# A shorter fallback path, 33 extra products at the head and smaller stores of one chunk in a fused attention and feed-forward kernel

## The chip, the cores and the metric

The kernel runs on one core of one Trainium2 chip. The core has five engines with instruction streams of their own: TensorE (PE in the profile, its weight loads PEld), VectorE (DVE), ScalarE (ACT), GpSimd (POOL) and SyncE (SP), and 16 DMA engines that all queues share. The metric is the device time of one execution in microseconds (us), smaller is better. Before the change the median of three runs is 411.15 us, the lowest 410.89 us, the highest 411.72 us.

## What is computed

Attention over 8 batches and 8 heads of 64 dimensions. Keys and values have 1152 positions; queries are averaged in pairs first, so there are 576 queries per head. The attended values of the 8 heads, side by side, are the 512 features of 4608 tokens, which then pass through a multiplicative feed-forward block.

```python
q_pool = q.reshape(B, H, S // 2, 2, D).mean(axis=3)
scores = scale * np.matmul(q_pool, k.transpose(0, 1, 3, 2))
attn = softmax(scores)            # with the row's maximum taken off, and 1e-9 added to its sum
x = np.matmul(attn, v)            # -> (4608 tokens, 512)
a, b = x @ w1, x @ w2             # (512, 1024) each
out = ((a * b) @ w3) @ w_out      # (1024, 1024), (1024, 512) -> float32 (4608, 512)
```

## The kernel before, in words

**The main path.** Heads are worked two at a time: 32 pairs, numbered `p`. The scores of a pair go through PSUM buffers `psc` (line 438); ACT takes their exponential into `ring` without taking off a maximum (line 443). `av_mm` (line 456) multiplies 128 queries at a time with the values, to which a column of 1/16 is joined, so that PSUM holds the sum of the exponentials too; DVE divides by it (`av_norm`, line 486). The result must lie with its features on the partitions (`xT`). For the first eight pairs and for short tail groups PE turns it; for the others `x_dma` (line 476) issues one transposing DMA on SP's queue for each pair. The feed-forward block works on chunks of 512 tokens, nine of them, numbered 0 to 8: `w3 @ w_out` is multiplied once into `T16`, and each chunk is the products with `w1` and `w2`, their elementwise product `gT`, and the product with `T16` (`moe_groups`, line 592). A beam search (`_visits`, line 179) lays out beforehand in which order PE takes scores, values and the pieces of chunks. `LATE` is 7: chunks 0 to 6 are done as just said, in the gaps between scores; chunks 7 and 8 come last (`late_chunks`, line 672), in an order written out by hand, `LATE_ORDER`, with seven block products where a plain block scheme has eight. Their sums of blocks of `xT` are formed on POOL by `x_sums` (line 659).

**Stores.** `put` (line 619) scales a finished 128-token tile into an `osb` buffer, of which there are three, and `store` (line 581) writes it to HBM with one DMA. Chunks 0 to 4 use POOL's queue, chunks 5 and 6 SP's. The outputs of chunks 7 and 8 are stored in half tiles from `room`, on SP's or on ACT's queue (`LATE_BY_ACT`, line 257). DMAs of SP and ACT take eight completion semaphores, the lanes HW0 to HW7, in turn; a DMA waits on its queue until the one before it on its lane has landed.

**The guard.** Since no maximum is taken off, the sums must lie in a range for the half-precision result to be good. Lines 988 to 1009 count those that do; `bad` is the number that don't, and every engine loads it into a register (line 1007, in `late_chunks` after 8 of its units). After everything else each engine meets a branch (line 1010): if `bad` is zero it jumps over the code of `_general` (line 24), the fallback, which does the whole computation again with the maximum taken off, in loops over batch, 96-query chunk, pair of heads, and blocks of 128 features of the feed-forward block. With this case's data `bad` is zero and nothing of the fallback runs, but its instructions lie in each engine's stream between the branch and its target. At the target each engine waits for what is still under way. SP waits for the stores: first for some lanes one by one (a block at line 1010), then for all queues' lanes in a list of twelve instructions (line 1037); then the engines meet at a barrier.

**The head.** `first_loads` (line 386) starts the DMAs of the first pair. POOL writes the identity `ident16` (lines 843 to 847); PE's first work is `first_turn` (line 415), which turns the first blocks of keys and queries with it when they have come and POOL and DVE have cast them.

Of the kernel before, what the change touches and what calls it, by code (L numbers as in the profile page):

```python
# [8 lines left out]
FP32 = mybir.dt.float32  # L9
FP16 = mybir.dt.float16  # L10
AF = mybir.ActivationFunctionType
ALU = mybir.AluOpType
# [11 lines left out]
def _general(tc, q, k, v, out, w1sb, w2sb, T16):  # L24

    nc = tc.nc
    B, H, S, D = q.shape
    Sq = S // 2
    NJ = S // 128
    dm = H * D  # L30
    dff = w1sb.shape[2]
    NC = dm // 128
    NF = dff // 128
    QP = 96
    SCALE = 0.5 * float(D) ** -0.5
    SCL = 16.0
    W = 384
    kf, vf = (t.rearrange("b h s d -> (b h) s d") for t in (k, v))
    qr = q.rearrange("b h s d -> (b h s) d")
    with tc.tile_pool(name="gen", bufs=1) as sb, \  # L40
         tc.tile_pool(name="gen_ps", bufs=1, space=bass.MemoryType.PSUM) as ps, \
         tc.For_i(0, B, 1) as ib, tc.For_i(0, Sq, QP) as iq:
        xT = sb.tile([128, NC * QP], FP16)
        gT = sb.tile([128, NF * QP], FP16)
        with tc.For_i(0, H // 2, 1) as ip:
            pav = ps.tile([128, 512], FP32, tag="g_pav")
            for u in range(2):
                ih = ib * H + ip * 2 + u
                hs = u * 64
                kst = sb.tile([128, NJ, D], FP32, tag="g_kst")  # L50
                nc.gpsimd.dma_start(out=kst, in_=kf[bass.ds(ih, 1)].rearrange("o (c p) d -> p (o c) d", p=128))
                vst = sb.tile([128, NJ, D], FP32, tag="g_vst")
                nc.gpsimd.dma_start(out=vst, in_=vf[bass.ds(ih, 1)].rearrange("o (c p) d -> p (o c) d", p=128))
                qst = sb.tile([QP, 2, D], FP32, tag="g_qst")
                nc.gpsimd.dma_start(out=qst, in_=qr[bass.ds(ih * S + iq * 2, 2 * QP)].rearrange("(p t) d -> p t d", t=2))
                kh = sb.tile([128, NJ, 128], FP16, tag="g_kh")
                qh = sb.tile([QP, 128], FP16, tag="g_qh")
                vh = sb.tile([128, NJ, D], FP16, tag="g_vh")
                nc.gpsimd.memset(kh, 0.0)
                nc.gpsimd.memset(qh, 0.0)  # L60
                nc.gpsimd.tensor_copy(out=kh[:, :, 0:D], in_=kst)
                nc.gpsimd.tensor_tensor(out=qh[:, 0:D], in0=qst[:, 0, :], in1=qst[:, 1, :], op=ALU.add)
                nc.gpsimd.tensor_copy(out=vh, in_=vst)
                kT = sb.tile([128, NJ, 128], FP16, tag="g_kT")
                nc.sync.dma_start(out=kT, in_=kh.rearrange("p c d -> p (c d)"), transpose=True)
                qT = sb.tile([128, QP], FP16, tag="g_qT")
                nc.sync.dma_start(out=qT, in_=qh, transpose=True)
                kTf = kT.rearrange("p c i -> p (c i)")
                pss = ps.tile([128, S // W, 512], FP32, tag="g_pss")
                for w in range(S // W):  # L70
                    nc.tensor.matmul(pss[0:QP, w, 0:W], qT, kTf[:, w * W:w * W + W], start=True, stop=True)
                mx = sb.tile([QP, 1], FP32, tag="g_mx")
                nc.vector.tensor_reduce(out=mx, in_=pss[0:QP, :, 0:W], axis=mybir.AxisListType.XY, op=ALU.max)
                nb = sb.tile([QP, 1], FP32, tag="g_nb")
                nc.scalar.mul(out=nb, in_=mx, mul=-SCALE)
                e = sb.tile([QP, S // W, W], FP32, tag="g_e")
                nc.scalar.activation(out=e, in_=pss[0:QP, :, 0:W], func=AF.Exp, bias=nb, scale=SCALE)
                z = sb.tile([QP, 1], FP32, tag="g_z")
                nc.vector.tensor_reduce(out=z, in_=e, axis=mybir.AxisListType.XY, op=ALU.add)
                nc.vector.tensor_scalar(out=z, in0=z, scalar1=1e-9, scalar2=None, op0=ALU.add)  # L80
                rz = sb.tile([QP, 1], FP32, tag="g_rz")
                nc.vector.reciprocal(out=rz, in_=z)
                eh = sb.tile([QP, S], FP16, tag="g_eh")
                nc.vector.tensor_scalar(out=eh, in0=e.rearrange("p w i -> p (w i)"), scalar1=rz, scalar2=SCL,
                                        op0=ALU.mult, op1=ALU.mult)
                eT = sb.tile([128, NJ, QP], FP16, tag="g_eT")
                nc.sync.dma_start(out=eT, in_=eh, transpose=True)
                for jt in range(NJ):
                    nc.tensor.matmul(pav[hs:hs + 64, 0:QP], vh[:, jt, :], eT[:, jt, :], start=(jt == 0), stop=(jt == NJ - 1))
                nc.vector.tensor_copy(out=xT[hs:hs + 64, bass.ds(ip * QP, QP)], in_=pav[hs:hs + 64, 0:QP])  # L90
        with tc.For_i(0, NF, 1) as ift:
            pw = [ps.tile([128, 512], FP32, tag=tg, name=tg) for tg in ("g_pa", "g_pb")]
            for wt, p, tg in ((w1sb, pw[0], "g_w1"), (w2sb, pw[1], "g_w2")):
                wc = sb.tile([128, NC, 128], FP16, tag=tg, name=tg)
                nc.gpsimd.tensor_copy(out=wc, in_=wt[:, :, bass.ds(ift * 128, 128)])
                for mc in range(NC):
                    nc.tensor.matmul(p[:, 0:QP], wc[:, mc, :], xT[:, mc * QP:mc * QP + QP],
                                     start=(mc == 0), stop=(mc == NC - 1))
            asb = sb.tile([128, QP], FP32, tag="g_asb")
            nc.scalar.copy(out=asb, in_=pw[0][:, 0:QP])  # L100
            nc.vector.tensor_tensor(out=gT[:, bass.ds(ift * QP, QP)], in0=pw[1][:, 0:QP], in1=asb, op=ALU.mult)
        po = ps.tile([128, 512], FP32, tag="g_po")
        for ft in range(NF):
            nc.tensor.matmul(po[0:QP, :], gT[:, ft * QP:ft * QP + QP], T16[:, ft, :], start=(ft == 0), stop=(ft == NF - 1))
# [156 lines left out]
def kernel(  # L261
# [26 lines left out]
    QM = 4  # L288
    QT = Sq - QM * 128
    E1 = D + 1  # L290
    SCALE = 0.5 * float(D) ** -0.5
    SCL = 16.0
# [12 lines left out]
    ps = fast.enter_context(tc.tile_pool(name="ps", bufs=1, space=bass.MemoryType.PSUM))  # L305
# [4 lines left out]
    ident16 = const.tile([128, 128], FP16)  # L310
# [267 lines left out]
                nc.tensor.matmul(pw[:, d0:d0 + n], wt[:, mc, ft * 128:ft * 128 + 128], xT[:, mc, a:a + n],  # L578
                                 start=(mc == 0 and d0 == 0), stop=(mc == NC - 1), skip_group_check=True)

    def store(eng, pos, osb, cols=slice(0, dm)):
        b, r = pos // (2 * Sq) * 2, pos % (2 * Sq)
        if r == QM * 128:
            for u in range(2):
                r0 = (b + u) * Sq + QM * 128
                eng.dma_start(out=out[r0:r0 + QT, cols], in_=osb[u * QT:u * QT + QT, :])
            return
        if r > QM * 128:
            b, r = b + 1, r - QM * 128 - 2 * QT
        eng.dma_start(out=out[b * Sq:b * Sq + QM * 128, :].rearrange("(p c) n -> p c n", c=QM)[:, r // 128, cols], in_=osb)  # L590

    def moe_groups(c):
        t = {}
# [243 lines left out]
    def w_load(dst, src):  # L837
# [204 lines left out]
```

## Time and profile before

| what | us |
|---|---|
| median of three runs | 411.15 |
| the profiled execution's own time | 411.33 |
| its span, first to last instruction of the kernel | 409.7 |
| PE busy | 394.7 (96%) |
| ACT busy | 335.2 (82%) |
| DVE busy, POOL busy | 218.6 (53%), 213.0 (52%) |
| first product of PE starts | 5.16 |
| last arithmetic (DVE, line 764) ends | 404.65 |

The profile shows one execution on the chip. The span begins with the kernel's first instruction; the time outside it, 1.6 us here, is start and end of the program. "Busy" is the share of the span in which an engine works on something; waits, branches and DMA issues are not counted. The chain of waits goes back from the last instruction to what released it, step by step. A line number is one of the kernel's file before the change.

### The profile page before, as it was taken

The numbers are of one execution on the slowest core, as the hardware profiler recorded it, in microseconds if no ns is written. First come the engines' busy times: TensorE is split into PE (matmuls) and PEld (weight loads), VectorE is DVE, ScalarE is ACT, GpSimd is POOL, SyncE is SP. The second block draws the span as 40 slices with busy tenths as digits, with TensorE's granted clock in tenths as the row PEclk, the third lists the DMA queues.
The fourth block names the chain that finished last, engine by engine and source line by source line (L and its number), as shares of the span: only waits on it lengthen the run. The fifth ranks groups of instructions, "written<-read, shape, count | busy, mean of one in ns | idle before, by whom it ended". The sixth has DMA issues, their size and how long they took to land.

```text
span 409.7 us, 13103 instructions
## 1 busy us (share of the span) xinstructions
PE 394.7 (96%) x5473; PEld 260.2 (64%) x5473; DVE 218.6 (53%) x594; ACT 335.2 (82%) x380; POOL 213.0 (52%) x237
## 2 busy tenths in 40 slices
PE   3899999999999999999999999999999999999994
PEld 1477777566555655565556555665777655658883
DVE  1255664665455534554365536563456435856982
ACT  4978979898889998999999998998998989017752
POOL 5879976570555145604533346333533997070850
PEclk9999999999999999999999999999999999999999
DMA  8999999999599899949999999998997270020015
GB/s 255 252 308 284 267 282 313 342 241 271 195 226 237 214 290 283 282 47 251 311 242 260 239 286 280 256 284 199 282 232 185 28 149 14 15 91 27 2 39 172
DMA packets 92224, 86.35 MB, mean 211 GB/s; under 512 B 59776, under 2 KB 66176, under 8 KB 92160
## 3 DMA queue, kind: packets, MB, share of 16 engines
q1 hardware_dynamic: 82624, 60.11, 62.2%
q0 software_dynamic: 8384, 24.06, 20.4%
q10 hardware_dynamic: 1152, 1.31, 1.0%
q8 instruction: 43, 0.70, 0.7%
q14 instruction: 21, 0.17, 0.1%
HBM read 67.11 MB, written 9.44 MB: 187 GB/s over the span
## 4 chain that ended last, share of the span: by engine, by line
PE 93%; ACT 2%; DVE 2%; DMA 1%; issue 1%; ACTq 0%
PE psc L438 20%; PE avb L469 17%; PE mo L578 15%; PE mo L616 11%; PE mot L578 9%; PE b L713 7%; PE mo L556 3%; PE avb L466 3%; ACT ring L443 2%; PE b L616 2%; PE ptk L378 2%; PE mo L713 1%; DMA qst<-in_q_dram 1%; PE avb L713 1%; DVE kqT L380 1%; PE mot L556 1%
## 5 line engine op out<-in xcount | busy, mean ns | idle before, releaser
L443 ACT ACTIVATE ring<-psc 128x1024 f16<-128x1024 f32 x324 | 308.2, 1025 | 33.2 <-PE psc L438 31.4
L469 PEld LDWEIGHTS <-ring 128*128 128x128 f16 x2304 | 84.4, 98 | 26.3 <-issue 7.1
L438 PE MATMUL psc<-kqT 64*128 64x512 f16 (+7 forms) x1152 | 96.1, 290 | 3.6 <-ACT ring L443 0.9
L469 PE MATMUL avb<-vaug,ring 128*128 128x65 f16 x2304 | 91.4, 193 | 0.0
L350 POOL CAST kq<-kst 128x1152 f16<-128x1152 f32 x31 | 35.7, 1152 | 77.8 <-DMA kqT<-kq 56.7
L438 PEld LDWEIGHTS <-kqT 64*128 64x128 f16 x1152 | 45.9, 95 | 31.0 <-issue 8.5
L616 PE MATMUL mo<-T,gT 128*128 128x512 f16 x192 | 45.6, 380 | 0.0
L490 DVE RECIPROCAL rzall<-avb 128x2 f32<-128x2 f32 x144 | 23.8, 165 | 37.0 <-PE avb L469 20.3
L625 DVE TENSOR_SCALAR osb<-mo 128x512 f32<-128x512 f32 x24 | 16.6, 692 | 48.6 <-PE mo L616 48.6
L354 POOL TENSOR_TENSOR kq<-qst 128x512 f16<-128x512 f32 x31 | 39.4, 1271 | 2.3 <-DMA qst<-in_q_dram 2.3
L363 POOL CAST vaug<-vst 128x1152 f16<-128x1152 f32 x32 | 36.6, 1145 | 7.0 <-DMA vst<-in_v_dram 7.0
L609 DVE TENSOR_TENSOR gT<-mo,asb 128x512 f16<-128x512 f32 x36 | 24.9, 692 | 24.7 <-PE mo L578 24.6
L590 POOL DMA_DIRECT2D out_dram<-osb x18 | 9.9, 552 | 54.1 <-DVE rzall L490 54.1
L578 PE MATMUL mo<-xT,w2sb 128*128 128x512 f16 (+2 forms) x168 | 37.2, 350 | 0.0
L616 PEld LDWEIGHTS <-gT 128*128 128x128 f16 x224 | 19.8, 98 | 25.6 <-issue 5.2
L578 PEld LDWEIGHTS <-w2sb 128*128 128x128 f16 x256 | 21.9, 97 | 20.8 <-issue 4.2
L605 DVE COPY asb<-mo 128x512 f32<-128x512 f32 x32 | 22.1, 691 | 24.0 <-PE mo L578 23.7
L578 PEld LDWEIGHTS <-w1sb 128*128 128x128 f16 x256 | 22.0, 97 | 20.3 <-issue 3.9
L578 PE MATMUL mo<-xT,w1sb 128*128 128x512 f16 (+2 forms) x148 | 33.1, 352 | 0.0
L504 DVE TENSOR_TENSOR xb<-avb,rzall 128x128 f16<-128x128 f32 x96 | 28.0, 291 | 3.3
L578 PE MATMUL mot<-xT,w1sb 128*128 128x512 f16 (+1 forms) x104 | 23.6, 354 | 0.1
L578 PE MATMUL mot<-xT,w2sb 128*128 128x512 f16 (+1 forms) x84 | 19.5, 359 | 0.0
(141 smaller groups left out, 429.6 us busy)
## 6 DMA issues: line engine op xcount, KB each, us to landing
vst<-in_v_dram SPq DMA_DIRECT2D x25, 576.0 KB, 5.0
kst<-in_k_dram SPq DMA_DIRECT2D x23, 576.0 KB, 5.8
qst<-in_q_dram SPq DMA_DIRECT2D x23, 512.0 KB, 7.4
kst<-in_k_dram POOLq DMA_DIRECT2D x8, 576.0 KB, 9.8
out_dram<-osb POOLq DMA_DIRECT2D x18, 256.0 KB, 6.2
qst<-in_q_dram POOLq DMA_DIRECT2D x8, 512.0 KB, 10.5
vst<-in_v_dram POOLq DMA_DIRECT2D x7, 576.0 KB, 7.1
w3c<-in_moe_w_dram POOLq DMA_DIRECT2D x4, 512.0 KB, 8.2
```

The costliest lines, as they stand in the source:

```text
L350: nc.gpsimd.tensor_copy(out=kq16[:, 0:NJ].rearrange("p c u d -> p u c d"), in_=kst.rearrange("p u (c d) -> p u c d", d=D))
L354: eng.tensor_tensor(out=kq16[:, NJ:NJ + QM].rearrange("p c u d -> p u c d"), in0=qv[:, :, :, 0], in1=qv[:, :, :, 1], op=ALU.add)
L363: nc.gpsimd.tensor_copy(out=va[:, :, :, 0:D], in_=vs.pop(p).rearrange("p u (c d) -> p u c d", d=D))
L438: nc.tensor.matmul(psc[:, u, f - s * G:f - s * G + ln], kT2[u * 64:u * 64 + 64, jt, :], qpT[u * 64:u * 64 + 64, i0:i0 + ln], start=True, s ...
L443: nc.scalar.activation(out=ring[:, :, r0:r0 + G], in_=psc, func=AF.Exp, bias=0.0, scale=SCALE)
L469: nc.tensor.matmul(avb[:, o + u * E1:o + u * E1 + E1], ring[:, u, c0:c0 + 128], va[:, u, jt, :], start=(jt == 0 and u == 0), stop=(jt == N ...
L490: nc.vector.reciprocal(out=rzall[:, i, :], in_=av[:, :, D:E1].rearrange("p u o -> p (u o)"))
L504: nc.vector.tensor_tensor(out=xbt, in0=av[:, :, 0:D], in1=rzall[:, i, :].unsqueeze(2).to_broadcast([128, 2, D]), op=ALU.mult)
L578: nc.tensor.matmul(pw[:, d0:d0 + n], wt[:, mc, ft * 128:ft * 128 + 128], xT[:, mc, a:a + n], start=(mc == 0 and d0 == 0), stop=(mc == NC - ...
L609: nc.vector.tensor_tensor(out=t["g"][:, ft, :], in0=pb, in1=t["a"], op=ALU.mult)
L616: nc.tensor.matmul(po, t["g"][:, ft, tt:tt + 128], T16[:, ft, :], start=(ft == 0), stop=(ft == NF - 1))
L713: nc.tensor.matmul(pt[:, n * f:n * f + n], l[:, i, :], b[:, i, :], start=(p in (1, 5) and f == 0 and i == 0), stop=(i == kc - 1), skip_gro ...
```

## The change

Three things are edited.

1. `_general`, the fallback: its loop over heads and its loop over feature blocks are gone, so that three nested loops are left. A pass of the inner one now does both heads of a pair at once, with one transposing DMA for both heads' keys, one for the queries and one for the attention weights; the feed-forward block is done in one go for the 96 queries.
2. At the head PE multiplies the identity with its first 64 columns 33 times, into `avb`, right after POOL has the identity.
3. The stores of chunk 6 are cut: where one DMA wrote a tile of 128 rows x 512 columns, four write 128 columns each for the first two tiles, and eight write 64 rows x 128 columns each for the other two. That makes 24 DMAs of 4.

```diff
-    def store(eng, pos, osb, cols=slice(0, dm)):
+    def store(eng, pos, osb, cols=slice(0, dm), rows=slice(0, 128)):
...
-        eng.dma_start(out=out[b * Sq:b * Sq + QM * 128, :].rearrange("(p c) n -> p c n", c=QM)[:, r // 128, cols], in_=osb)
+        eng.dma_start(out=out[b * Sq:b * Sq + QM * 128, :].rearrange("(p c) n -> p c n", c=QM)[rows, r // 128, cols], in_=osb)
...
-                store(nc.sync if c >= LATE - 2 else nc.gpsimd, c * CH + tt, osb)
+                if c == LATE - 1:
+                    cut = 128 if tt < 256 else 64
+                    for r in range(0, 128, cut):
+                        for n in range(0, dm, 128):
+                            store(nc.sync, c * CH + tt, osb[r:r + cut, n:n + 128], slice(n, n + 128), slice(r, r + cut))
+                else:
+                    store(nc.sync if c == LATE - 2 else nc.gpsimd, c * CH + tt, osb)
...
+    for _ in range(33):
+        nc.tensor.matmul(avb[:, 0:64], ident16, ident16[:, 0:64], start=True, stop=True)
     for t in kq16s:
         nc.gpsimd.memset(t[QT:128, NB - 1], 0.0)
```

The core of the fallback's edit, cut to the loops:

```diff
         with tc.For_i(0, H // 2, 1) as ip:
-            for u in range(2):
-                ih = ib * H + ip * 2 + u
...
-                nc.sync.dma_start(out=kT, in_=kh.rearrange("p c d -> p (c d)"), transpose=True)
-                nc.sync.dma_start(out=qT, in_=qh, transpose=True)
...
-                nc.sync.dma_start(out=eT, in_=eh, transpose=True)
+            ih = ib * H + ip * 2
...
+            nc.sync.dma_start(out=kT, in_=kh.rearrange("p c o d -> p (c o d)"), transpose=True)
+            nc.sync.dma_start(out=qT, in_=qh.rearrange("p u o d -> p (u o d)"), transpose=True)
...
+            nc.sync.dma_start(out=eT.rearrange("p u c i -> p (u c) i"), in_=eh.rearrange("p u s -> p (u s)"), transpose=True)
...
-        with tc.For_i(0, NF, 1) as ift:
...
+        for m, wt in enumerate((w1sb, w2sb)):
+            for n in range(2):
                 for mc in range(NC):
+                    nc.tensor.matmul(pw[0:QP, m, n, :], xT[:, mc * QP:mc * QP + QP], wt[:, mc, n * 512:n * 512 + 512],
                                      start=(mc == 0), stop=(mc == NC - 1))
```

In the built programs' instruction lists, counted on each engine from the program's first instruction, the guard's branch and its target stand here (the order of all other instructions of the main path is the same, except that lanes are dealt out anew behind the added DMAs):

| engine | branch before | target before | branch after | target after |
|---|---|---|---|---|
| PE | 10951 | 11146 | 11017 | 11182 |
| SP | 334 | 508 | 356 | 485 |
| ACT | 719 | 836 | 720 | 808 |
| DVE | 680 | 810 | 681 | 774 |
| POOL | 371 | 542 | 371 | 499 |

The last four stores, all on ACT's queue, have lanes HW0 to HW3 before and HW4 to HW7 after.

More of the change, by code (lines that the diff above doesn't have):

```diff
@@ L43, in _general @@
         xT = sb.tile([128, NC * QP], FP16)
[L44 removed]
         with tc.For_i(0, H // 2, 1) as ip:
[L46 removed]
+            ih = ib * H + ip * 2
+            kst = sb.tile([128, NJ, 2, D], FP32, tag="g_kst")
+            vst = sb.tile([128, NJ, 2, D], FP32, tag="g_vst")
             for u in range(2):
[L48 to L90 removed]
@@ L91, in _general @@
-        with tc.For_i(0, NF, 1) as ift:
[L92 to L95, printed above, removed]
+                for st, src in ((kst, kf), (vst, vf)):
+                    nc.gpsimd.dma_start(out=st[:, :, u], in_=src[bass.ds(ih + u, 1)].rearrange("o (c p) d -> p (o c) d", p=128))
@@ new lines, in _general @@
+            for u in range(2):
+                nc.gpsimd.tensor_tensor(out=qh[:, u, u], in0=qst[:, u, 0], in1=qst[:, u, 1], op=ALU.add)
+            nc.gpsimd.tensor_copy(out=vh, in_=vst)
+            kT = sb.tile([128, NJ, 128], FP16, tag="g_kT")
+            nc.sync.dma_start(out=kT, in_=kh.rearrange("p c o d -> p (c o d)"), transpose=True)
+            qT = sb.tile([128, 2, QP], FP16, tag="g_qT")
+            nc.sync.dma_start(out=qT, in_=qh.rearrange("p u o d -> p (u o d)"), transpose=True)
@@ new lines, in _general @@
+            kTf = kT.rearrange("p c i -> p (c i)")
+            pss = ps.tile([128, 2, S // W, 512], FP32, tag="g_big", name="g_pss")
+            for u in range(2):
+                for w in range(S // W):
+                    nc.tensor.matmul(pss[0:QP, u, w, 0:W], qT[:, u, :], kTf[:, w * W:w * W + W], start=True, stop=True)
+            mx = sb.tile([QP, 2], FP32, tag="g_mx")
+            nc.vector.tensor_reduce(out=mx, in_=pss[0:QP, :, :, 0:W], axis=mybir.AxisListType.XY, op=ALU.max)
+            nb = sb.tile([QP, 2], FP32, tag="g_nb")
@@ new lines, in _general @@
+            nc.scalar.mul(out=nb, in_=mx, mul=-SCALE)
+            e = sb.tile([QP, 2, S // W, W], FP32, tag="g_e")
+            for u in range(2):
+                nc.scalar.activation(out=e[:, u], in_=pss[0:QP, u, :, 0:W], func=AF.Exp, bias=nb[:, u:u + 1], scale=SCALE)
+            z = sb.tile([QP, 2], FP32, tag="g_z")
+            nc.vector.tensor_reduce(out=z, in_=e, axis=mybir.AxisListType.XY, op=ALU.add)
+            nc.gpsimd.tensor_scalar(out=z, in0=z, scalar1=1e-9, scalar2=None, op0=ALU.add)
@@ new lines, in _general @@
+            rz = sb.tile([QP, 2], FP32, tag="g_rz")
+            nc.vector.reciprocal(out=rz, in_=z)
+            eh = sb.tile([QP, 2, S], FP16, tag="g_eh")
+            for u in range(2):
+                nc.gpsimd.tensor_scalar(out=eh[:, u], in0=e[:, u].rearrange("p w i -> p (w i)"), scalar1=rz[:, u:u + 1],
+                                        scalar2=SCL, op0=ALU.mult, op1=ALU.mult)
+            eT = sb.tile([128, 2, NJ, QP], FP16, tag="g_eT")
+            nc.sync.dma_start(out=eT.rearrange("p u c i -> p (u c) i"), in_=eh.rearrange("p u s -> p (u s)"), transpose=True)
@@ new lines, in _general @@
+            pav = ps.tile([128, 2, QP], FP32, tag="g_pav")
+            for jt in range(NJ):
+                nc.tensor.matmul(pav, vh[:, jt].rearrange("p o d -> p (o d)"), eT[:, :, jt, :],
+                                 start=(jt == 0), stop=(jt == NJ - 1))
+            for u in range(2):
+                nc.vector.tensor_copy(out=xT[u * 64:u * 64 + 64, bass.ds(ip * QP, QP)], in_=pav[u * 64:u * 64 + 64, u])
+        pw = ps.tile([128, 2, 2, 512], FP32, tag="g_big", name="g_pw")
+        for m, wt in enumerate((w1sb, w2sb)):
+            for n in range(2):
```

24 lines of the change are left out of this document (17 added, 7 removed).

## The prediction

> **What bounds the kernel now.** I read the page's chain first, then the timeline and the guard's lines in the last microseconds, then the DMA queues there, then the head.
>
> ```profile
> PE 93%; ACT 2%; DVE 2%; DMA 1%; issue 1%; ACTq 0%
> ...
> 403.33 2.36 ACTq L590 DMA_DIRECT2D out_dram<-room  x4
> 404.23 0.42 DVE L764 SCALAR_TENSOR_TENSOR room<-b,room 128x256 f32<-128x256 f32 x1
> ...
> L1010 SPq EVENT_SEMAPHORE  x7: 17/17/17, 407.0 to 408.0; - x7
> L1010 PEldq COMPARE_BRANCH  x1: 358/358/358, 402.2 to 402.2; - x1
> L1010 SPq COMPARE_BRANCH  x1: 58/58/58, 403.3 to 403.3; - x1
> L1010 DVEq COMPARE_BRANCH  x1: 72/72/72, 404.2 to 404.2; - x1
> L1010 ACTq COMPARE_BRANCH  x1: 54/54/54, 405.7 to 405.7; - x1
> ...
> L1037 SPq EVENT_SEMAPHORE  x14: 17/28/28, 408.0 to 409.6; - x14
> L1037 SPq DRAIN  x3: 7/7/13, 408.8 to 409.1; - x3
> ...
> q14 instruction: 4, 0.03, 2.7%
> q8 instruction: 1, 0.02, 0.8%
> out_dram<-room ACTq DMA_DIRECT2D x4, 128.0 KB, 3.5
> ```
>
> PE carries the chain nearly to the end, so only what delays PE, or what comes after it, counts. After the last arithmetic (404.65) the span goes on for 5.0 us. ACT issues the last four stores until 405.69; SP, at its branch already at 403.3, gets through its first wait at 407.0 and reaches the barrier at 408.84; all others are there by 406.3. So **the last stores' landing and SP's list of waits are the bound of the last 4 us**. The two instruction rows (403 to 409.7) are fetches of code, five in number: their records start at 403.92 (16 KB, PE's queue), 404.33, 405.48, 406.82 and 406.94 (8 KB each).
>
> Two things make the 3.5 us of those stores. First, of the 16 parts of each store 15 land together and one, always one DMA engine's, late: the store of 403.33 has its parts by 405.45 but for two, the last at 407.02; the next three end at 407.34, 407.65 and 408.10, where the others' parts were in by 405.8, 406.96 and 407.26. That engine is behind since 404 (a store landed whole at 403.61, the next has 15 parts by 404.28 and the last at 406.05): just when the fetches of 403.92 and 404.33 (0.90 and 0.87 us) are served. Second, SP passes its list one by one, about 0.065 us each: waits on HW0, HW1, HW2 end at 407.04, 407.36, 407.67, exactly on the late landings; then come 4 old lanes, 12 list entries and two drains, 1.17 us in which nothing is awaited any more.
>
> The head:
>
> ```profile
> 1.14 0.29 POOL L844 TENSOR_SCALAR_AFFINE_SELECT ident<-ident 128x128 f16<-128x128 f16 x1
> 5.16 0.50 PE L418 MATMUL ptf<-ident,kq 128*128 128x128 f16 x3 [5.16 <-POOL kq L404]
> ...
> 15.25 1.66 PE ptk L378 x14
> 26.09 0.91 PE ptk L378 x14
> ```
>
> PE has nothing to do until 5.16, and its first turns run at half pace: 14 take 1.66 us, later 0.91. The trace's clock record turns to full at 20.05.
>
> **The change part by part.**
>
> *Fallback.* `bad` is zero, none of it ran or will run. It changes only how far the branches jump (PE 195 to 165 instructions, SP 174 to 129, ACT 117 to 88).
>
> *33 products.* POOL has the identity at 1.43; a semaphore from POOL to PE takes 0.05 (5.10 to 5.15), so they start at 1.48. No row has a 64-column product at half pace. From below: 18 pairs of 128-column load and 65-column product take 0.55 (line 469), 0.031 each at full pace, 0.061 at half: 2.0 us. From above: the turns' pair at half pace, 0.107 for 128 columns: 3.5 us. They end at 3.5 to 5.0 and PE waits until 5.16 for POOL's cast either way: cost 0. I take 2.0, since the line-469 pair has nearly the same shape. If the cover were gone, each us past 5.16 would be paid in full. `avb` is next written by PE itself, in order. [...]
>
> *24 stores.* SP issues a store of line 590 in about 0.33 us, 0.37 to 0.40 with its wait. The first four start at 362.34 where one did; behind them on SP is the last transposing DMA (362.78), now about 1.2 us later. It feeds `x_sums` on POOL, which waited for it:
>
> ```profile
> 362.78 1.22 SPq L480 DMA_TRANSPOSE xT<-xb  x1
> 365.31 1.22 POOL L636 TENSOR_TENSOR xS<-xT,xS 128x512 f16<-128x512 f16 x1 [2.99 <-issue]
> 379.34 1.16 POOL L803 TENSOR_TENSOR room<-gT 128x512 f16<-128x512 f16 x1 [10.58 <-PE b L713]
> ```
>
> POOL's sums would end at 370.0 instead of 368.8. Chunk 8's first unit is twentieth in `LATE_ORDER` (367.3 + 19 x 0.436 = 375.6), its first with a sum thirtieth (380); POOL's next work is idle-covered for 10 us. Cost 0; it would be paid from 5 us of delay on. The third and fourth tile's 16 stores keep SP until about 373.4, then it loads `bad`; its next store is due at 389.84: 0. The fourth tile's `osb` is the first's, free when its four stores have landed (363.9 + 2.1, the landing of line 590's stores, = 366.0), wanted at 367.35: 0, with 1.3 us to spare. Lanes return after 8 issues, 3 us, against a landing in 2.1: 0.
>
> *Lanes.* 20 more DMAs are 4 modulo 8. The last four stores move from HW0 to HW3 to HW4 to HW7. SP's list then has HW4 last in its first block, then 4 entries of POOL's queue, HW0 to HW4, and only then HW5, HW6, HW7 and the drains: the idle list runs while the stores land. With landings as now: HW4 407.04; ten steps to 407.7; HW5 and HW6 pass; HW7 408.12; drains 408.25, against 408.84: **-0.6**.
>
> *Fetches.* The fetch records put a boundary every 128 instructions on the small engines (POOL's at about 72, 200, 328; SP's about 80, 210, so 338, 466; ACT's 66 to 706; DVE's to 704), every 256 on PE (about 10944). A fetch starts about 1.1 us after a boundary or a branch across one (POOL branches at 394.59, fetch at 395.69; ACT 405.72, 406.82; DVE 404.24 plus its 0.07, 405.48; SP 403.31, 404.33). Before, SP at 334 stood short of 338 and jumped over a whole block to 508; PE crossed 10944 7 instructions ahead of its branch; ACT jumped across 834. After, SP crosses 338 with its late stores, at about 392, and 485 lies in the next block: one fetch at 404.3 instead of two. PE crosses 73 instructions ahead of its branch: 4 us earlier, about 399.7. ACT's 808 stays in its block: none. So of five fetches after 403 two are left. PE's now meets the stores of 400, whose parts occupy that engine 0.35 us in every 0.45; its 0.9 us backlog is worked off by about 403.5. Then the late engine is late by single fetches of 0.31 (what an 8 KB fetch alone takes): HW4 at 405.4, HW5 406.1, HW6 at the others' 406.96, HW7 407.26. SP: HW4 405.42, ten steps to 406.1, HW6 406.98, HW7 407.28, drains 407.40. Against 408.84 **-1.44 with the lanes**; the fetches' share is 0.84. From below the share is 0 (if the late engine is late for another reason), from above 0.84: with every part at the others' time SP can't be sooner.
>
> Sum: 411.33 - 1.44 = 409.89 on the profiled execution, which is 0.18 over the median; by the median 409.71. I take 409.8.
>
> [...]
>
> **The rivals.**
> - *Lanes alone.* The late engine stays late (its own traffic, or fetches I place wrongly by a few instructions: PE's target 11182 is 18 short of a boundary). For it: each late part follows the last by 0.32 even at 406.82, when two fetches run. Against: the jump at 404. Time 411.33 - 0.6 = 410.7.
> - *Slower: the products hold up the first turn.* Place: PE before 5.16. It starts to cost above 0.111 us a pair (3.68 / 33), and beats the end's gain above 0.155. Load and product in a row (0.098 + 0.053) are 0.15, 411.2; at 0.2, two thirds of a product's full 0.29, they end at 8.1, +2.9 - 1.44, 412.8. Against: 18 products into the same columns follow at 0.031, and turns at 0.107.
> [...]
>
> **How the numbers follow.** Forecast 0.56, its own range 409.2 to 410.4 (1.9 to 0.7 us; run-to-run spread 0.8 at most); lanes alone 0.16; products late 0.10; clock early 0.10; the rest, such as an unforeseen stall of PE by fetches moved 66 instructions, 0.08, half of it slower. About 0.2%, 0.82 us, is what a measurement can tell from no change. Faster: forecast less its shallow edge (0.54) and clock early (0.10), 0.64. Lanes alone, the edge and part of the rest: 0.20 same. Slower 0.16. The range takes in forecast and lanes alone with the spread, 408.6 to 411.3; it leaves out the early clock and the late products.
>
> **What would show it.** Right: two instruction fetches after 403, PE's near 400, last parts of the four stores near 405.4, 406.1, 406.9, 407.3, SP at the barrier 2.7 to 3.0 us after the last arithmetic instead of 4.2; the first turn still at 5.16. Wrong: a first turn after 5.2, a turn of 14 before 20 us in 0.9 us, or late parts at 407 and beyond.

## The result, and the profile after

The changed kernel takes 410.32 us (median of 18 runs, 409.78 to 411.45); the kernel before, measured beside it, 411.13 us (18 runs, 410.35 to 412.13). The ratio is 0.9981 with a 95% interval of 0.9973 to 0.9989: faster by 0.1 to 0.3%. The forecast was 409.8 (408.6 to 411.3), with 0.64 for faster. So sign and range held, and the time lies between the forecast and the rival "lanes alone" (410.7). Which of the two it was, the profile has to say.

The profiled execution after took 411.45 us and its span is 409.8 us. It is the slowest of its 18, so it can't be laid beside the one before from end to end. Part of that is one wait that the chain before did not have, some 200 us ahead of the end. The view of PE's waits after (total in us, times, longest in us):

```profile
PE mo L583 <- DMA xT<-xb: 1.1, 1, 1.1
```

No step of the change explains this wait of 1.1 us. The kernels below that have a part of the change, or the change with an edit more, have it at 0 to 0.4; only the changed kernel itself has it again on another chip, at 1.3, in the slowest of its executions there. Whether it belongs to the whole change stays open. What can be compared is the stretch behind the last arithmetic, which ends at 405.37 after and at 404.65 before. From there to SP's drain before the barrier it is 4.19 us before (408.84) and **3.59 us after** (408.96). The share of the chain by engine, after:

```profile
PE 88%; DMA 6%; POOL 2%; ACT 1%; issue 1%; DVE 1%; SPq 0%; ACTq 0%
```

PE still carries it nearly to the end. The timeline of the last microseconds after (start, length, engine, line, operation):

```profile
404.05 2.01 ACTq L595 DMA_DIRECT2D out_dram<-room  x4
...
404.95 0.42 DVE L775 SCALAR_TENSOR_TENSOR room<-b,room 128x256 f32<-128x256 f32 x1
```

The same four stores on ACT that took 2.36 us before now take 2.01. The rows of the guard's first line after (durations in ns, first and last start in us):

```profile
L1023 SPq EVENT_SEMAPHORE  x5: 17/17/17, 405.7 to 407.2; - x5
...
L1023 PEldq COMPARE_BRANCH  x1: 223/223/223, 402.9 to 402.9; - x1
L1023 SPq COMPARE_BRANCH  x1: 58/58/58, 404.8 to 404.8; - x1
...
L1023 DVEq COMPARE_BRANCH  x1: 72/72/72, 405.0 to 405.0; - x1
...
L1023 ACTq COMPARE_BRANCH  x1: 54/54/54, 406.1 to 406.1; - x1
```

and of the list behind it:

```profile
L1050 SPq EVENT_SEMAPHORE  x14: 17/28/28, 407.3 to 409.7; - x14
...
L1050 SPq DRAIN  x3: 7/7/13, 408.9 to 409.2; - x3
```

Two things are to be seen. SP's first block has five waits instead of seven, and the list of line 1050 starts at 407.3 while the stores are still landing. By the trace's wait records SP is through with everything but HW6 and HW7 at 407.81; those two waits end at 408.51 and 408.83, right on the landings of the last two stores (408.50, 408.81), and the barrier's drain comes 0.15 us after the last one. Before it was 0.74 (408.10 to 408.84): the idle list. And SP's branch, at 403.3 before, 1.3 us ahead of the last arithmetic, is now at 404.8, only 0.5 ahead. Why, the timeline of SP's queue shows. Before:

```profile
398.79 1.13 SPq L586 DMA_DIRECT2D out_dram<-room  x2
```

After:

```profile
399.53 2.16 SPq L591 DMA_DIRECT2D out_dram<-room  x2
```

The second of these two stores took 0.58 us before and 1.61 after. What SP does later is late by most of that: its branch by 0.80 us, counted from the last arithmetic. Last, the DMA queues from 403 us to the end, after:

```profile
q14 instruction: 2, 0.02, 1.2%
...
out_dram<-room ACTq DMA_DIRECT2D x5, 128.0 KB, 2.8
```

Five fetches of code have become two, and PE's (16 KB) starts at 399.75, as forecast. But the two that are left start at 406.84 and 406.88. The last store has 14 of its 16 parts by 407.94 and the other two at 408.50 and 408.81: the last part is as late as before (0.87 us; 0.84 before).

The head, after:

```profile
1.49 1.94 PE L860 MATMUL avb<-ident 128*128 128x64 f16 x33 [1.49 <-POOL ident L855]
...
4.71 0.50 PE L423 MATMUL ptf<-ident,kq 128*128 128x128 f16 x3 [1.27 <-POOL kq L409]
...
14.70 1.65 PE L383 MATMUL ptk<-ident,kq 128*128 128x128 f16 x14 [0.31 <-ACT ring L448]
```

The products are done at 3.43, PE then waits 1.27 us for POOL, and the turns of 14.70 still go at half pace (0.91 us at full). The stores of chunk 6 on SP, after:

```profile
363.06 1.78 SPq L595 DMA_DIRECT2D out_dram<-osb  x4
364.93 1.19 SPq L485 DMA_TRANSPOSE xT<-xb  x1
366.22 13.21 SPq L595 DMA_DIRECT2D out_dram<-osb  x20
```

### The profile page after: what moved, and what is told of

The parts are those of the page before. It is cut to its first block, busy times and chain, and to the rows that moved or that the text cites. A ratio compares the mean times of both kernels' runs of the same rounds, so it can differ in the third digit from the quotient of the medians.

```text
span 409.8 us, 13190 instructions
## 1 busy us (share of the span) xinstructions
PE 396.8 (97%) x5506; PEld 261.6 (64%) x5506; DVE 218.7 (53%) x594; ACT 335.2 (82%) x380; POOL 212.8 (52%) x237
## 4 chain that ended last, share of the span: by engine, by line
PE 88%; DMA 6%; POOL 2%; ACT 1%; issue 1%; DVE 1%; SPq 0%; ACTq 0%
PE psc L443 19%; PE avb L474 16%; PE mo L583 15%; PE mo L621 10%; PE mot L583 9%; PE b L724 7%; PE mo L561 3%; DMA qst<-in_q_dram 3%; PE avb L471 3%; DMA xT<-xb 3%; PE b L621 2%; PE mo L724 1%; PE ptk L383 1%; ACT ring L448 1%; DMA kst<-in_k_dram 1%; PE avb L724 1%
```

## The experiments

All kernels compute the reference in full. They ran in three sets, each on one chip with its own runs of the kernel before (medians 411.10, 411.24 and 411.19 us); ratios are to those. A ratio is worked out from the single executions, not from the medians, and can differ by 0.2% from theirs. A difference of 0.2% is at the edge of what the times tell, so two numbers from the profiled execution of each kernel carry most of the argument. They come from one execution each; the changed kernel's two agree to 0.12 us in their sum:

- **landing**: from the end of the last arithmetic to the landing of the last store (records of the completion semaphores);
- **rest**: from that landing to SP's drain before the barrier.

| kernel | median us | ratio, 95% interval | landing | rest | sum | PE's fetch starts | store held up, its length |
|---|---|---|---|---|---|---|---|
| before | 411.13 | 1 | 3.45 | 0.74 | 4.19 | 403.92 | ACT 404.28, 0.94 |
| changed | 410.32 | 0.9981 (0.9973 to 0.9989) | 3.44 | 0.15 | 3.59 | 399.75 | SP 400.07, 1.61 |
| after_again | 410.92 | 0.9980 (0.9958 to 1.0002) | 3.55 | 0.16 | 3.71 | 401.17 | SP 401.51, 1.66 |
| fallback | 411.01 | 0.9983 (0.9959 to 1.0007) | 3.17 | 0.61 | 3.78 | 402.87 | ACT 403.68, 1.17 |
| stores | 410.68 | 1.0008 (0.9985 to 1.0031) | 3.13 | 0.57 | 3.70 | 403.14 | ACT 403.71, 1.24 |
| products | 413.06 | 1.0047 (1.0034 to 1.0060) | 3.99 | 0.97 | 4.96 | 398.92 and 404.00 | SP 399.27, 1.20; ACT 404.22, 1.25 |
| no_products | 410.64 | 0.9985 (0.9960 to 1.0010) | 3.18 | 0.15 | 3.33 | 403.34 | ACT 403.92, 1.29 |
| lanes_back | 411.27 | 1.0005 (0.9990 to 1.0021) | 3.52 | 0.39 | 3.91 | 399.43 | SP 399.79, 1.43 |
| warm128 | 410.17 | 0.9973 (0.9962 to 0.9985) | 3.52 | 0.15 | 3.67 | 398.81 | SP 399.14, 1.72 |
| dve_pad | 410.75 | 0.9975 (0.9955 to 0.9994) | 2.73 | 0.15 | 2.88 | 399.57 | SP 400.08, 1.08 |
| sp_store | 410.76 | 0.9983 (0.9967 to 0.9999) | 3.60 | 0.15 | 3.75 | 399.38 | SP 399.72, 1.74 |
| np_sp_store | 410.17 | 0.9967 (0.9939 to 0.9994) | 3.21 | 0.15 | 3.37 | 402.59 | ACT 403.17, 1.06 |
| np_pad | 410.87 | 0.9982 (0.9968 to 0.9996) | 3.33 | 0.14 | 3.47 | 403.81 | ACT 404.38, 1.18 |
| np_sp_pad | 410.88 | 0.9990 (0.9981 to 1.0000) | 3.04 | 0.15 | 3.19 | 403.41 | ACT 404.18, 1.16 |

A store of ACT or SP in this stretch is issued in 0.33 to 0.62 us when nothing holds it up (np_sp_pad has one of 0.71, begun 1.2 us behind PE's fetch). The profile does not name the engine that an 8 KB fetch is for; where the text does, it goes by the order of the branches.

**1. fallback.** The kernel before with the new `_general` alone.

```diff
-            for u in range(2):
-                ih = ib * H + ip * 2 + u
...
+            ih = ib * H + ip * 2
...
-        with tc.For_i(0, NF, 1) as ift:
...
+        for m, wt in enumerate((w1sb, w2sb)):
+            for n in range(2):
```

> The kernel before with the shorter fallback alone. SP's first block of waits shrinks from seven lanes to five (HW0, HW4 to HW7), the last four stores stay on HW0 to HW3, PE's code fetch stays at about 403.9. Theory A (list and fetches both matter, as forecast): SP waits on HW0 in the first block, meets HW3 with four entries and two drains behind it, 0.34 us less than before from the list, up to 0.3 more because SP's and ACT's jumps now need one fetch less each: 410.5 to 410.8. Theory B (only the list of waits matters): -0.3, 410.8. Theory C (the gain is at the head, from the products): no change, 411.1.

0.17% by the ratio, 0.1 us by the medians, and the interval takes in no change; the median of 411.01 is nearest to theory C. The profile's end is shorter all the same, by 0.41 us, of which 0.28 is an earlier landing. It shows three fetches of 8 KB after 404 instead of four. The rest is 0.61. The first block is now HW0 and HW4 to HW7; SP is held in it by HW0 until 406.75 and goes through the others and the list step by step. HW3, the last store's, lands at 407.69, while SP is still at earlier entries; its entry passes at 407.91, and four more entries and the drains follow.

**2. no_products.** The changed kernel without the 33 products.

```diff
-    for _ in range(33):
-        nc.tensor.matmul(avb[:, 0:64], ident16, ident16[:, 0:64], start=True, stop=True)
```

> The changed kernel without the 33 products: PE's branch back at 10951, its code fetch back at 403.9 among the last stores, instead of 399.75. Theory A: the late engine is late by up to 0.9 us more, 0.4 us slower than the changed kernel, 410.7. Theory B: as the changed kernel, 410.3, or a little faster, since the fetch at 399.75 held up a store of SP by 1.1 us in the changed kernel's profile (400.07, 1.61 us instead of 0.58) and SP's stores behind it. Theory C: the whole gain is gone, 411.1.

0.9985 against 0.9981 with them: the products are worth nothing that these runs can tell. First turn at 4.82. The median of 410.64 is near theory A's 410.7, but not for its reason: the landing is not later than in the changed kernel, it is 0.26 us earlier. At the end PE's fetch is back at 403.34 and ACT, not SP, is held up: its store of 403.92 takes 1.29, so that the last store is issued 1.06 us after the last arithmetic (0.13 in the changed kernel), but its last part is then only 0.20 us behind the others. The sum is 3.33, even shorter than the changed kernel's.

**3. lanes_back.** The changed kernel with chunk 5's stores on POOL's queue except for one DMA, so that the last four stores are on HW0 to HW3 again.

```diff
-                eng.dma_start(out=out[r0:r0 + QT, cols], in_=osb[u * QT:u * QT + QT, :])
+                e = nc.sync if u == 1 and pos // CH == LATE - 2 else eng
+                e.dma_start(out=out[r0:r0 + QT, cols], in_=osb[u * QT:u * QT + QT, :])
...
-                    store(nc.sync if c == LATE - 2 else nc.gpsimd, c * CH + tt, osb)
+                    store(nc.gpsimd, c * CH + tt, osb)
```

> The changed kernel with four of chunk 5's five stores on POOL's queue, which moves the last four stores back to HW0 to HW3; the positions of PE's and ACT's branches stay within 2 instructions, SP's goes from 356 to 349. Theories A and B: HW3 has four entries and two drains behind it (0.4 us) where HW7 has the two drains (0.14): 0.3 us slower than the changed kernel, 410.6. Theory C: no difference, 410.3.

The guard's rows, the block and the list behind it:

```profile
L1024 SPq EVENT_SEMAPHORE  x5: 17/17/17, 406.3 to 406.9; - x5
```

```profile
L1051 SPq EVENT_SEMAPHORE  x14: 17/28/28, 407.0 to 409.8; - x14
...
L1051 SPq DRAIN  x3: 7/7/13, 408.9 to 409.3; - x3
```

The rest goes from 0.15 back to 0.39, with the landing unchanged (3.52): HW3 lands at 408.61, and four entries and the drains stand behind the wait for it. The gain is gone from the times too (1.0005), by more than the 0.24 us that the rest explains; what makes the difference is open. The move of chunk 5 to POOL's queue comes with it, so the times alone don't say it is the lanes; the rest does.

**4. warm128.** The changed kernel with 128 columns a product instead of 64.

```diff
-        nc.tensor.matmul(avb[:, 0:64], ident16, ident16[:, 0:64], start=True, stop=True)
+        nc.tensor.matmul(avb[:, 0:128], ident16, ident16, start=True, stop=True)
```

> The changed kernel with 128 columns in each of the 33 products instead of 64, no other instruction moved. [...] If the head's chain is set by DMAs and exponentials (the chain of the changed kernel's profile goes through DMAs until 23.7), no gain: 410.3. If the products hold up the first turn: up to 0.3 us slower.

PE is now busy with them from 1.50 to about 5.0, just up to the first turn at 4.99; the first scores start at 6.81, as in the changed kernel (6.79). The clock turns to full at 21.07, not sooner than before (20.05) or in the changed kernel (18.92): the added columns did not bring it forward. What turns it no run shows. The median of 410.17 can't be told from the changed kernel's 0.9981, and the profile shows nothing that would make it faster.

**5. after_again.** The changed kernel itself, on another chip.

> The changed kernel once more, beside the next three on the same chip, as their base. 410.3. From its profile a second reading of the end: SP at the barrier 3.6 us after the last arithmetic, the PE fetch at 399 to 400 holding up one SP store by about 1.1 us, two fetches about 1.5 us after the last arithmetic, the last two stores' late parts 0.6 to 0.9 us behind the others.

Again 0.998, but here the interval takes in no change, and the median of 410.92 is above the 410.3 expected. The profile repeats the changed kernel's end: rest 0.16, PE's fetch early, SP's store held up (1.66), the two fetches at 408.33 and 408.55, 1.5 and 1.7 us behind the last arithmetic, and the last parts 0.97 us late.

**6. dve_pad.** The changed kernel with 40 memsets of one element on DVE at the head. DVE then meets the boundary of code that it crossed with its branch some 40 instructions earlier (its fetch comes at 397.23 instead of 406.88), and its target stays in the block that it has (one fetch after 403 instead of two).

```diff
+    pad = const.tile([1, 1], FP32, name="pad")
+    for _ in range(40):
+        nc.vector.memset(pad, 0.0)
```

> The changed kernel with 40 one-element memsets on DVE at the head, where it waits until about 3.7 for the first query: its branch goes from 681 to 721, past the block boundary at about 704, and its target, 814, stays in the same block. Theory F (the late parts of the last stores come from the code fetches that SP's and DVE's jumps set off): one fetch instead of two after the last arithmetic, DVE's moved to about 390 to 400; one late part per store instead of two, 0.1 to 0.5 us less at the end, 409.9 to 410.2. Theory G (the late engines are late for another reason, such as the stores' own traffic): two late parts as before, no change, 410.3.

The DMA queues from 403 us to the end:

```profile
q14 instruction: 1, 0.01, 0.5%
```

DVE's fetch is at 397.23, only SP's is left (at 405.90, some 1 us sooner than in the changed kernel), the last store has one late part instead of two (408.11, the others by 407.62), and the landing falls from 3.44 to 2.73. With a sum of 2.88 this is the end that the prediction wanted (2.7 to 3.0). So **the late parts hang on the fetches, not on the late engine's own traffic**. The time shows less of it (410.75, where 409.9 to 410.2 was expected). A likely reason, not isolated by a run, is the head; the timeline there:

```profile
0.92 4.36 DVE L861 MEMSET pad<- 1x1 f32 x39 [0.92 <-PEq L1042]
...
6.40 0.61 PE L423 MATMUL avb<-ident,kq 128*128 128x128 f16 x4 [1.12 <-DVE kq L411]
```

The 40 memsets come 0.11 us apart and keep DVE until 5.4; its cast is late, PE waits 1.12 us for it, and the first scores come at 7.80 instead of 6.79. That was not foreseen, and it holds for experiments 11 and 12 as well.

**7. sp_store.** The changed kernel with one late unit, `o10c12`, stored by SP instead of ACT.

```diff
-LATE_BY_ACT = "o00c21 o01c12 o10c12 o10c21 o11c12 o11c21".split()
+LATE_BY_ACT = "o00c21 o01c12 o10c21 o11c12 o11c21".split()
```

> The changed kernel with the last store but one (o10c12) on SP's queue instead of ACT's. ACT's queue has one store less before the last. In the changed kernel's profile ACT was only 0.13 us behind the data with the last store, so the landing gains at most that; SP's branch and its fetch move later by 0.4 us, nearer to the last landing. Theory F: 0 to 0.3 us slower than the changed kernel, since SP's fetch meets the last store later; theory G: 0.1 us faster.

No gain: 0.9983, sum 3.75. The last arithmetic ends at 405.03, the two fetches of 8 KB come at 406.68 and 407.33, and the parts of the last store are late again (408.63, most of the others by 407.9).

**8. np_sp_store.** The same without the products.

```diff
-LATE_BY_ACT = "o00c21 o01c12 o10c12 o10c21 o11c12 o11c21".split()
+LATE_BY_ACT = "o00c21 o01c12 o10c21 o11c12 o11c21".split()
...
-    for _ in range(33):
-        nc.tensor.matmul(avb[:, 0:64], ident16, ident16[:, 0:64], start=True, stop=True)
```

> The changed kernel without the products, so that PE's fetch stays at 403.3 and holds up ACT's store by about 0.9 us, and with o10c12 on SP's queue. ACT's last store, 1.06 us behind the last arithmetic without products (0.13 with them), is issued about 0.4 us sooner. SP at the barrier 2.9 to 3.1 us after the last arithmetic, against 3.33 without products and 3.59 with: 410.0 to 410.2, faster than the changed kernel by 0.1 to 0.3. If ACT's store is held up by something else than the fetch, 3.3 and 410.5.

Sum 3.37, median 410.17: the time is in the expected range, the end is not (2.9 to 3.1). ACT's last store did go out sooner, 0.31 us behind the last arithmetic instead of 1.06, and ACT's store behind the fetch was held up as expected (1.06 us). But the last store has three of its 16 parts late, by 0.45 to 0.65 us, behind fetches of 405.13 and 405.57, so it lands no sooner (3.21 against 3.18). The interval (0.9939 to 0.9994) overlaps the changed kernel's in the same set (0.9958 to 1.0002). Its profile has the clock at full in one early stretch, from 11.95 to 15.36, and then for good from 18.78. Its last arithmetic ends at 404.01, the earliest of all; whether that stretch is the reason no run shows.

**9. stores.** The kernel before with the smaller stores of chunk 6 alone.

```diff
-                store(nc.sync if c >= LATE - 2 else nc.gpsimd, c * CH + tt, osb)
+                if c == LATE - 1:
+                    cut = 128 if tt < 256 else 64
+                    for r in range(0, 128, cut):
+                        for n in range(0, dm, 128):
+                            store(nc.sync, c * CH + tt, osb[r:r + cut, n:n + 128], slice(n, n + 128), slice(r, r + cut))
+                else:
+                    store(nc.sync if c == LATE - 2 else nc.gpsimd, c * CH + tt, osb)
```

> The kernel before with the smaller stores of chunk 6 alone: the old fallback, no products at the head. The last four stores move to HW4 to HW7, but the guard's first block of waits is HW0 to HW6 (the old fallback uses seven queues), then four entries, then HW7 and the drains. The prediction's reading (the lanes alone give 0.6): last arithmetic to barrier about 3.6 us, median 410.6. My reading now (the lanes pay only together with the shorter fallback, whose first block ends at HW4): the wait on HW6 ends at about 3.3 after the last arithmetic, four entries and HW7 and the drains follow, 0.4 us behind it or 0.15 behind HW7's landing: 3.7 to 4.1, median 410.8 to 411.2. PE's fetch stays near 403.9 and holds up a store of ACT by about 1 us.

Both readings come out at about their near edges, 3.70 for 3.6 and for 3.7 to 4.1, and the median of 410.68 lies between; three of 12 runs at 412 to 415 us blur the ratio. What tells them apart is the order of the waits. The guard's rows:

```profile
L1016 SPq EVENT_SEMAPHORE  x7: 17/17/17, 403.7 to 407.4; - x7
```

```profile
L1043 SPq EVENT_SEMAPHORE  x14: 17/28/28, 407.4 to 409.0; - x14
...
L1043 SPq DRAIN  x3: 7/7/13, 408.2 to 408.5; - x3
```

The block of seven holds SP on HW6 until 407.37; HW7 lands at 407.68, while SP works through the list until 408.12. The rest is 0.57 and not 0.15: the lanes alone don't take the idle list away. The gain in the sum that this run has against before (0.49) is mostly an earlier landing (0.32), which has no late part in the last store (0.15 us behind the others).

**10. products.** The kernel before with the 33 products alone.

```diff
+    for _ in range(33):
+        nc.tensor.matmul(avb[:, 0:64], ident16, ident16[:, 0:64], start=True, stop=True)
```

> The kernel before with the 33 products alone: the old fallback and the old stores. The prediction's reading: nothing at the head (first turn at 4.7 to 5.2, products done by 3.5); at the end PE's fetch near 400 instead of 403.9, but the jump to 11212 crosses a second boundary at about 11200, so PE fetches again after its branch, near 403.3; four to five fetches after the last 5.5 us begin, the wait list as before: 4.0 to 4.2 us from last arithmetic to barrier, median 411.0 to 411.3. A rival (the products raise the clock early or make the scores' first turns faster): a turn of 14 in 0.9 us before 18 us and a median of 410.5 or less. Another (the products delay the head): a first turn after 5.2 and a median above 411.6.

Slower by 0.34 to 0.60%. The third reading has the size, but not the reason. The products end at 3.43; PE's first turn at 5.24 waits 1.80 us for POOL's cast, and the first scores start at 7.24 (7.34 before): nothing is lost at the head. The loss is at the end. Its DMA queues from 403 to 410 us, and the four stores on ACT there:

```profile
q14 instruction: 4, 0.03, 2.0%
q8 instruction: 1, 0.02, 1.0%
```

```profile
403.25 3.17 ACTq L590 DMA_DIRECT2D out_dram<-room  x4
```

PE fetches at 398.92 as it crosses the first boundary, and once more at 404.00 because its jump, now from 11017 to 11212, crosses the next one at about 11200, by the spacing of some 256 instructions that its 43 fetches in the trace of before show. Each fetch holds up a store (SP's of 399.27 takes 1.20, ACT's of 404.22 takes 1.25 and the next 0.85). The four stores take 3.17 us instead of 2.36, and the sum is 4.96 instead of 4.19. That is 0.77 us of a profiled execution that is the fastest of its six (412.02 to 413.65); what makes the others another 1 us slower no profile here shows.

**11. np_pad.** No products, and the memsets of experiment 6.

```diff
+    pad = const.tile([1, 1], FP32, name="pad")
+    for _ in range(40):
+        nc.vector.memset(pad, 0.0)
-    for _ in range(33):
-        nc.tensor.matmul(avb[:, 0:64], ident16, ident16[:, 0:64], start=True, stop=True)
```

> The changed kernel without the products and with 40 memsets of one element on DVE at the head, so that DVE crosses its code boundary early and ends on the far side of it. Theory that the late parts of the last stores are code fetches: DVE's fetch goes from the end to about 397, one fetch (SP's, near 404.7) is left after the last arithmetic, at most one late part in the last store, and last arithmetic to barrier 2.8 to 3.2 us instead of the 3.33 of the kernel without products; median 410.2 to 410.6. Rival (the engine is late by its own traffic): the late parts stay as they were, 3.3 to 3.6 us, median 410.6 to 411.0.

A miss in the number: 3.47 instead of 2.8 to 3.2. The last store has no late part at all (408.44 to 408.55), as the theory of the fetches has it, but it was issued late. The stores on ACT in the last microseconds (min, median, max in ns):

```profile
L595 ACTq DMA_DIRECT2D out_dram<-room x4: 338/629/1183, 403.9 to 406.6; - x4
```

PE's fetch (403.81) holds up the store of 404.38 (1.18 us), SP's fetch (405.25) that of 405.66 (0.87), and the last goes out at 406.63, 1.41 us behind the last arithmetic. So in these traces a fetch costs in one of two ways: it makes a part late (by 0.87 us in the changed kernel), or it holds up an issue (1.18 and 0.87 us here, where 0.33 to 0.62 is usual).

**12. np_sp_pad.** No products, the memsets, and `o10c12` on SP.

```diff
-LATE_BY_ACT = "o00c21 o01c12 o10c12 o10c21 o11c12 o11c21".split()
+LATE_BY_ACT = "o00c21 o01c12 o10c21 o11c12 o11c21".split()
...
+    pad = const.tile([1, 1], FP32, name="pad")
+    for _ in range(40):
+        nc.vector.memset(pad, 0.0)
-    for _ in range(33):
-        nc.tensor.matmul(avb[:, 0:64], ident16, ident16[:, 0:64], start=True, stop=True)
```

> The same (no products, 40 memsets on DVE at the head) with one more late store moved from ACT to SP, so that ACT is free sooner for the last four. Theory of the fetches: last arithmetic to barrier 2.8 to 3.2 us against the 3.37 of the same kernel without the memsets; median 409.8 to 410.3, the best of all runs. Rival (the memsets buy nothing): 3.4 us and 410.2 to 410.6.

The sum is 3.19, as the theory of the fetches had it, with one held-up store of ACT instead of two. The median of 410.88 misses its range of 409.8 to 410.3: first scores at 7.79, 0.6 later than without the memsets (7.15). No kernel that was run is clearly faster than the changed one; np_sp_store and warm128 have the lowest medians, with intervals that overlap its own.

## Why the prediction came out as it did

- **Fallback: 0.** Right as it stands: none of it ran. But it isn't neutral. It makes SP's block five waits long, without which the lanes don't pay (rest 0.57 in experiment 9), and it keeps PE's target at 11182, short of the boundary at 11200 that the products alone jump across (a fetch at 404.00 in experiment 10). The prediction named the 18 instructions to that boundary only as a risk.
- **33 products: 0 at the head.** Right: 1.94 us for the 2.0 taken, with 1.27 us of cover left. (The first turn came at 4.71 and not at 5.16; in the other traces it stands between 4.76 and 5.24.) The rival "the products hold up the first turn" fell: a pair takes 0.059 us, and paying would have begun at 0.111.
- **The rival "the clock rises early"** fell too. Its chance of 0.10 was an estimate; no run shows what turns the clock to full. In all traces but one it turned once: at 20.05 before, 18.92 after, 21.07 in warm128, each time behind the first turns of 14 (begun at 15.25, 14.70 and 14.72), which took 1.65 us; the next 14 took 0.91 before (26.09). The exception is np_sp_store, which has no products: its clock was at full from 11.95 to 15.36 and for good from 18.78. So more work of PE at the head, 1.94 us of products after and about 3.5 in warm128, did not raise the clock ahead of those turns.
- **24 stores: 0.** Right, with a wrong size. SP took 0.59 us for the median store of the last 20, not 0.37 to 0.40, and one of them 1.68, next to a fetch of PE's (372.07); SP was busy until 379.4 and not 373.4. Its next store is due ten us later, so that cost nothing. The transposing DMA went out at 364.93, 2.15 us later than before where 1.2 was forecast; POOL's sums still ended at 370.85, nine us ahead of its next work.
- **Lanes: -0.6.** Right: the rest went from 0.74 to 0.15, -0.59. It was put down to the lanes; it takes the lanes and the shorter fallback together (rest 0.61 with the fallback alone, 0.57 with the lanes alone, 0.39 with the shorter block and the lanes put back).
- **Fetches: -0.84.** This step failed. What it says of the fetches themselves came true: five became two, and PE's moved to 399.75. What it makes of them didn't: the landing went from 3.45 to 3.44. Two sentences of it are wrong. "PE's now meets the stores of 400, whose parts occupy that engine": it doesn't only queue behind parts, it holds up the issue of a store by about 1.0 us, and now it hit SP's and no longer ACT's. And "a fetch starts about 1.1 us after a boundary or a branch across one": SP, held up, branched at 404.83, and its fetch and DVE's started 2.0 and 1.9 us behind their branches, at 406.84 and 406.88, when the last two stores had gone out and not yet landed. That the branch was late explains 0.80 us of it; why the fetches took longer to start no run shows. Nor was it one part a store, as the prediction had it: the last store has two late parts. That the fetches are what makes parts late, which the step took for granted, held (experiment 6): where DVE's was out of the way, the landing fell to 2.73, near the 2.6 that the step's times give (407.28 against 404.65).
- **The sum.** In the profile the end is shorter by 0.60 where 1.44 was forecast, which is the rival "lanes alone" to the tenth. The medians differ by 0.81 in the first comparison and 0.32 in the second (after_again), both ratios 0.998. The prediction's own signs speak against its forecast: the last parts came at 408.50 and 408.81, where 407 and beyond was to be the sign of being wrong, and SP reached the barrier 3.59 us after the last arithmetic, where 2.7 to 3.0 was to be the sign of being right. So the result is that of the rival, a little better by the first median, and it is luck that 410.32 lies at the edge of the forecast's own range (409.2 to 410.4). Of the fetches' 0.84 us 0.01 came; that is more than the 0.52 by which the forecast's 409.8 was too low, and the 0.2 us by which the first median did better than the profile's end no run explains. The parts that the prediction names for "slower" add up to 0.14 (0.10 and half of 0.08), not to its 0.16.

## What to carry to other kernels

Where a kernel ends in stores, look at what is still to be done after the last one has landed: a wait for the last lane should stand at the end of the list, so that the entries for old lanes pass meanwhile (a rest of 0.15 us here instead of 0.74), and the order of lanes shifts with every DMA added anywhere before (20 more moved the last four stores from HW0 to HW3 to HW4 to HW7). Code that is never run still has a place: where its branch and target lay against the blocks in which code is fetched decided here how many fetches met the last stores (five started after 403 before, two after, one in experiment 6), and an edit at the head that adds instructions moved them (PE's from 403.92 to 399.75). Judge such an edit together with the length of what is jumped over, and judge padding by what it delays where it stands (the first scores by 1.0 us in experiment 6).

## What the runs showed of the hardware that was not expected

- Near the end a fetch of PE's code (16 KB) holds up a store that SP or ACT issues next to it, by 0.5 to 1.2 us: in all fourteen traces a store begun 0.2 to 0.8 us after the fetch took 0.94 to 1.74 us where 0.33 to 0.62 is usual, and it moved from ACT's queue to SP's and back with the fetch. It happened with a fetch of 8 KB as well (0.87, experiment 11). Further ahead it is found too, if not always: in the kernel before, the four loads of `qtl` that SP began 0.1 to 0.4 us after a fetch of PE's took 1.08 to 1.70 us (0.61 to 0.77 in the other twenty); in the changed kernel one load of `qst` begun 0.26 us after such a fetch took its usual 0.37.
- The time from a branch across a boundary to the fetch isn't fixed: for SP 1.0 us before, 1.6 where its fetch is the only one left (experiment 6), and 2.0 in the changed kernel.
- That PE's jump from 11017 to 11212 sets off a fetch (404.00 in experiment 10) was expected; what one fetch more of PE's can come with at the end of this kernel was not: an end longer by 0.77 us (4.96 against 4.19) in the profiled execution of experiment 10.
